# Paced opening loads and whole-piece weight decoding in an attention and two-layer MLP kernel

## The chip, the core and the metric

The kernel runs on one core of a Trainium2 chip. The metric is device time in microseconds (us) of one execution. The core has a matmul engine (TensorE: PE for its matmuls, PEld for its weight loads), VectorE (DVE), ScalarE (ACT), GpSimd (POOL) and SyncE (SP), which issues every DMA of this kernel. Each engine takes its instructions in the order written and stops at the first one whose inputs are not ready.

## The reference

Chunked attention, then two MLPs without biases, in float32:

```python
# attention: batch 4, 8 heads, 768 positions, head_dim 64; chunks of 32 queries
k_full = np.concatenate([mem_k, k_ctx], axis=2)      # 8 memory slots + 16 left + 32 + 8 right
scores = scale * np.matmul(q_c, k_full.transpose(0, 1, 3, 2))
a = np.exp(scores - scores.max(-1, keepdims=True)); a = a / (a.sum(-1, keepdims=True) + 1e-9)
out_c = np.matmul(a, v_full)
x = out.transpose(0, 2, 1, 3).reshape(3072, 512)
# first MLP (w_in 512x2048, w_out 2048x512)
x = np.maximum(x @ w_in, 0.0) ** 2 @ w_out
# second MLP, same sizes, own weights: g(h) = h * tanh(softplus(h))
y = g(x @ w_in2) @ w_out2
```

## The kernel before

**Work.** The 24 tiles of 128 positions are handled as 12 pairs p, four pairs to a superblock `sb` of 1024 tokens (three superblocks). Pairs 0 to 3 are computed in an opening of their own; pairs 4 to 11 are laid beside the first MLP's matmuls. Each MLP layer runs 24 steps, `s` = 0 to 23 for the first and 24 to 47 for the second; a step is one superblock against one eighth `j` of the 2048 hidden columns. Products follow a seven-product (Strassen-like) scheme, so a step has seven products P1 to P7 against w_in (42 matmuls) and, one step later, the products against w_out (48 matmuls, "units", in the first layer).

**One step.** P1 goes to bank a, P6 to b, P5 to c. ACT copies a to `u1`, DVE makes `u2 = b + u1`; then come two units of the step before, P2 (onto a), P7 (onto b), DVE's `u3 = b + u1` (line 835), more units, P4 (onto b), P3 (onto c). P2 has to wait for the copy of a (line 809), P7 for u2 (line 816), P4 for u3 (line 835), and the next step's P6 for DVE's c21 (line 843). Behind every product and unit stands a "point": `rest()` issues there whatever a plan has put at that point of the step (15 points a step).

**Weights.** Weights arrive as 8-byte words and are decoded on the chip: 32 pieces of 128 x 1024 values. Each piece is loaded and decoded in two halves of 512 columns. `rebias` (line 153, ACT) rescales the high words, `decode` (lines 160, 163, 164, DVE) clamps, shifts and adds the low bits. For a w_in piece `sums_w` (lines 175 to 179, DVE) adds the Strassen sums; `round_w` (line 201, ACT) and `split_w` (line 207, DVE) make the two parts that the matmuls use, and for the second layer `round_w2` and `split_w2` (lines 219, 226) write these to DRAM. Three raw buffers hold three halves. The plan string of `plan_w` has one letter for each of these and a bar for each point: `"Aa|D|d|RS|s|rL||||l"`.

**Order.** The scheduler is off (`tc.manual_schedule()`), so the order on each engine is that of the code. In the opening SP issues q, k, v and raw loads one behind the other without waits of the code's own, except where a tile is still in use. PE fills the gaps of the opening with dummy matmuls on `ones` (line 871). Attention beside the first layer puts eight small Exp activations a half (line 403) at two neighbouring points.

Of the kernel before, what the change touches and what calls it, by code (L numbers as in the profile page):

```python
# [26 lines left out]
NB = 512  # L27
# [31 lines left out]
def tile_chunk_attention_moe_moe2(  # L59
# [65 lines left out]
    halves = [(e, h) for e in order_w for h in range(2)]  # L125
    raw_t, val_t, w1_t, w2_t, hi_t = {}, {}, {}, {}, {}
    AHEAD = 3
# [6 lines left out]

    def flush():
        for to, src in waiting:
            nc.sync.dma_start(out=to, in_=src)
        waiting.clear()

    def load_raw(i):  # L140
        if i < len(halves):
            (layer, j, kind), h = halves[i]
            raw_t[i] = pool.tile([128, 512, 2], U32, tag=f"raw{i % AHEAD}", name="raw")
            src = (w1, w2)[layer][j, kind][:, 512 * h:512 * h + 512].bitcast(U32)
            later(raw_t[i], src.rearrange("p (a b) -> p a b", b=2))

    def rebias(e, h, tag):
        i = halves.index((e, h))
        if h == 0:
            flush()  # L150
            val_t[e] = pool.tile([128, 1024 if e[2] and not e[0] else 2048], FP32, tag=tag, name="val")
# [3 lines left out]
    def decode(e, h):  # L155
        i = halves.index((e, h))
        val = val_t[e][:, 512 * h:512 * h + 512]
        vb = val.bitcast(U32)
        low = raw_t.pop(i)[:, :, 0]
# [3 lines left out]
        nc.vector.tensor_scalar(out=vb, in0=vb, scalar1=3, scalar2=None, op0=ALU.logical_shift_left)  # L163
        nc.vector.scalar_tensor_tensor(  # L164
            out=vb, in0=low, scalar=29, in1=vb, op0=ALU.logical_shift_right, op1=ALU.bitwise_or
        )
        load_raw(i + AHEAD)

    def sums_w(e, half):
# [4 lines left out]
        if half == 0:  # L174
            nc.vector.tensor_tensor(out=s1, in0=a21, in1=a22, op=ALU.add)
            nc.vector.tensor_tensor(out=s2, in0=s1, in1=a11, op=ALU.subtract)
        else:
            nc.vector.tensor_tensor(out=s3, in0=a11, in1=a21, op=ALU.subtract)
            nc.vector.tensor_tensor(out=s4, in0=a12, in1=s2, op=ALU.subtract)
# [105 lines left out]
    def spare(sb, i):  # L285

        return f"{('xt', 'raw')[(sb - NSB) % 2]}{i % 3}"

    def load_apart(sb, o):
        xt_t[sb, o] = pool.tile([128, 2 * NB], FP32, tag=spare(sb - 1, 2 * o), name="xa")  # L290
# [793 lines left out]
```

## Time and profile before

| | us |
|---|---|
| median of 3 runs (1087.55 to 1092.18) | 1088.66 |
| the profiled execution's own run | 1090.82 |
| its span in the profile | 1089.0 |

The span is the time from the first to the last instruction in the profiled execution; 1.8 us of its run lie outside it. The opening ends at 56.2 us, where the first product of step 0 starts. In views of the profile, a row of the timeline gives start, duration, engine, source line, operation, what it writes and reads and, in brackets, the engine's idle time ahead of it and what ended that. "issue" there means that no semaphore in the profile ended the wait.

### The profile page before, as it was taken

How to read it: one execution, taken by the hardware profiler on the slowest of the kernel's cores; microseconds unless marked ns; L12 is line 12 of the kernel's file. 1: busy time of each engine (PE TensorE's matmuls, PEld its weight loads, DVE VectorE, ACT ScalarE, POOL GpSimd, SP SyncE). 2: the span in 40 equal slices, each digit the busy share in tenths (PEclk: the TensorE clock that was granted, in tenths of full speed). 3: DMA queues.
4: the chain of work that ended last, by engine and by line, in shares of the span. 5: the costliest groups of instructions: out<-in, count | busy, mean ns of one | idle time of the engine just before them, and what ended most of it. 6: DMA issues, size and time to landing. Idle time of an engine off the chain costs nothing.

```text
span 1089.0 us, 19893 instructions
## 1 busy us (share of the span) xinstructions
PE 1045.6 (96%) x7435; PEld 846.3 (78%) x7443; DVE 847.5 (78%) x1147; ACT 586.5 (54%) x1119; POOL 420.5 (39%) x327
## 2 busy tenths in 40 slices
PE   7878999998999999999999999999999999999998
PEld 4557777776778788788888888888888888888887
DVE  5786979969857676679999767787868878867777
ACT  2567765746675774557565654444364443453332
POOL 1223333332324343222232144545455454644443
PEclk9898998999999999999999999999999999999999
DMA  9556776789999998989999998999998899987452
GB/s 351 222 190 251 270 269 258 273 289 304 350 359 344 326 326 284 300 304 378 352 359 329 312 293 281 312 322 329 387 359 279 295 310 362 376 261 231 152 174 78
DMA packets 192143, 321.38 MB, mean 295 GB/s; under 512 B 13488, under 2 KB 151088, under 8 KB 188208
## 3 DMA queue, kind: packets, MB, share of 16 engines
q1 hardware_dynamic: 192048, 320.11, 84.4%
q8 instruction: 60, 0.98, 0.4%
q14 instruction: 35, 0.29, 0.1%
HBM read 228.04 MB, written 92.01 MB: 294 GB/s over the span
## 4 chain that ended last, share of the span: by engine, by line
PE 59%; DVE 5%; DMA 4%; ACT 2%; SPq 1%; issue 1%; DVEq 0%; ACTq 0%
PE banks L514 28%; PE banks L604 20%; PE banks L569 9%; DMA w_d<-hi 1%; PE banks L647 1%; DMA w_d<-val 1%; DMA xt<-xt_d 1%; DVE y L583 1%; SPq L253 1%; DMA w2s<-w_d 1%; DVE val L164 1%; DVE val L226 1%; DVE val L163 0%; SPq L267 0%; DMA w1s<-w_d 0%
## 5 line engine op out<-in xcount | busy, mean ns | idle before, releaser
L514 PE MATMUL banks<-x,w1s 128*128 128x512 f32 x2016 | 497.5, 393 | 17.4 <-ACT u L809 6.7
L514 PEld LDWEIGHTS banks<-x,w1s 128*128 128x128 f32 x2016 | 378.3, 189 | 103.8 <-DVE u L835 9.5
L528 POOL TENSOR_TENSOR g<-r,g 128x512 fp32r<-128x512 f32 x190 | 263.9, 1396 | 489.6 <-ACT g L527 361.7
L569 PE MATMUL banks<-g,w2s 128*128 128x512 f32 x1152 | 280.1, 393 | 7.0 <-DVE y L583 5.4
L569 PEld LDWEIGHTS banks<-g,w2s 128*128 128x128 f32 x1152 | 215.1, 188 | 57.2 <-DVE y L583 8.3
L592 DVE TENSOR_TENSOR m<-banks,m 128x1024 f32<-128x1024 f32 (+1 forms) x145 | 175.5, 1214 | 51.0 <-PE banks L604 45.8
L604 PE MATMUL banks<-g,w2s 128*128 128x512 f32 x828 | 206.4, 389 | 0.0
L604 PEld LDWEIGHTS banks<-g,w2s 128*128 128x128 f32 x828 | 155.4, 188 | 32.4
L527 ACT CAST g<-r 128x512 fp32r<-128x512 f32 x190 | 115.7, 621 | 27.8 <-DVE r L555 23.3
L583 DVE TENSOR_TENSOR y<-banks,y 128x512 f32<-128x512 f32 x168 | 111.5, 682 | 20.9 <-PE banks L569 20.6
L528 POOL TENSOR_TENSOR g<-more,g 128x512 fp32r<-128x512 f32 x47 | 66.8, 1425 | 63.0 <-ACT g L527 42.2
L533 ACT ACTIVATE r<-r 128x512 f32<-128x512 f32 x72 | 45.4, 630 | 54.7 <-DVE r L843 39.6
L537 ACT ACTIVATE r<-r 128x512 f32<-128x512 f32 x48 | 30.3, 632 | 72.1 <-DVE r L843 37.3
L534 ACT ACTIVATE r<-r 128x512 f32<-128x512 f32 x96 | 60.8, 633 | 3.1
L160 DVE TENSOR_SCALAR val<-val 128x512 f32<-128x512 f32 x64 | 38.6, 603 | 24.8 <-ACT val L153 24.6
L226 DVE TENSOR_TENSOR val<-val,hi 128x1024 f32<-128x1024 f32 (+1 forms) x32 | 35.5, 1109 | 24.0 <-ACT hi L219 23.7
L164 DVE SCALAR_TENSOR_TENSOR val<-raw,val 128x512 uint32<-128x512 uint32 x64 | 50.5, 788 | 2.2
L219 ACT CAST hi<-val 128x1024 fp32r<-128x1024 f32 (+1 forms) x32 | 30.5, 952 | 39.9 <-DVE val L164 18.8
L153 ACT ACTIVATE val<-raw 128x512 f32<-128x512 f32 x64 | 40.4, 672 | 21.1 <-DMA w_d<-val 9.9
L809 ACT COPY u<-banks 128x512 f32<-128x512 f32 x48 | 28.4, 592 | 41.4 <-PE banks L514 41.4
L417 POOL TENSOR_TENSOR p<-p,sum 128x512 f32<-128x512 f32 x22 | 27.6, 1273 | 43.1 <-DVE sum L414 17.6
L835 DVE TENSOR_TENSOR u<-banks,u 128x512 f32<-128x512 f32 x48 | 33.0, 688 | 14.2 <-PE banks L514 11.5
(88 smaller groups left out, 1035.5 us busy)
## 6 DMA issues: line engine op xcount, KB each, us to landing
w1s<-w_d SPq DMA_DIRECT2D x280, 256.0 KB, 6.0
w2s<-w_d SPq DMA_DIRECT2D x229, 256.0 KB, 5.9
raw<-w_dram SPq DMA_DIRECT2D x64, 512.0 KB, 5.8
w_d<-w1s SPq DMA_DIRECT2D x8, 1792.0 KB, 9.2
x<-xs_d SPq DMA_DIRECT2D x14, 1024.0 KB, 11.2
v<-v_dram SPq DMA_DIRECT2D x24, 512.0 KB, 7.6
xt<-xt_d SPq DMA_DIRECT2D x21, 512.0 KB, 8.3
k<-k_dram SPq DMA_DIRECT2D x24, 368.0 KB, 7.2
```

What stands on the lines that cost most here:

```text
L153: nc.scalar.activation(out=val, in_=high.bitcast(FP32), func=ACTF.Prelu, scale=REBIAS, alpha=NEGATIVE)
L164: nc.vector.scalar_tensor_tensor(out=vb, in0=low, scalar=29, in1=vb, op0=ALU.logical_shift_right, op1=ALU.bitwise_or)
L226: nc.vector.tensor_tensor(out=val, in0=val, in1=hi, op=ALU.subtract)
L514: nc.tensor.matmul(out=ps, lhsT=w[:, a, f:f + 128], rhs=x[:, xi, c, kk, :], start=start and i == 0, stop=stop and i == len(order) - 1, ski ...
L527: nc.scalar.copy(out=g[:, 0], in_=r)
L528: nc.gpsimd.tensor_tensor(out=g[:, 1], in0=r, in1=g[:, 0].bitcast(FP32), op=ALU.subtract)
L533: nc.scalar.activation(out=r, in_=h, func=ACTF.Relu)
L534: nc.scalar.activation(out=r, in_=r, func=ACTF.Square)
L569: nc.tensor.matmul(out=ps, lhsT=w[:, a, blk(f), d % 2 * 128:d % 2 * 128 + 128], rhs=g_t[s, (f, t)][:, c, :], start=i == 0, stop=i == len(o ...
L583: nc.vector.tensor_tensor(out=y, in0=ps, in1=y, op=ALU.add)
L592: engine.tensor_tensor(out=to, in0=in0, in1=in1, op=ALU.add)
L604: nc.tensor.matmul(out=bank(first + d), lhsT=w[:, a, 128 * d:128 * d + 128], rhs=g[:, c, :], start=i == 0 and blk not in ONTO, stop=i == 2 ...
```

## The change

Four things change together.

1. In the opening, from the seventh load on, SP first issues a DMA of one element that reads the third load ahead, and so waits until that load has landed; then it issues the load.
2. A weight piece is decoded whole, by instructions of 1024 columns. Its two raw halves lie in one fixed tile `raws` of four halves. The two loads of piece n+2 go out behind the decoding of piece n. `sums_w` needs three instructions for four, and two of its differences change sign (with T3, that they meet).
3. The plans put these instructions at other points: rebias alone at the first, limit two points later, the rest later by a point or two.
4. The Exps of a pair go to four points, four at each; normalisation and the store of a pair move a point or two later. First-layer g tiles use six buffers in a fixed rotation for seven in a ring, which frees room for `raws`.

```diff
-    AHEAD = 3
+    raws = const.tile([128, 4, 1024], FP32, name="raws")
...
-    def rebias(e, h, tag):
...
-        val, high = val_t[e][:, 512 * h:512 * h + 512], raw_t[i][:, :, 1]
-        nc.scalar.activation(out=val, in_=high.bitcast(FP32), func=ACTF.Prelu, scale=REBIAS, alpha=NEGATIVE)
+    def rebias(e, tag):
...
+        val = val_t[e][:, 0:1024].rearrange("p (h f) -> p h f", h=2)
+        high = raw_of(order_w.index(e)).rearrange("p h (f b) -> p h f b", b=2)[:, :, :, 1]
+        nc.scalar.activation(out=val, in_=high, func=ACTF.Prelu, scale=REBIAS, alpha=NEGATIVE)
...
-        load_raw(i + AHEAD)
+        beside_next.append(n + 2)
...
-            nc.vector.tensor_tensor(out=s1, in0=a21, in1=a22, op=ALU.add)
-            nc.vector.tensor_tensor(out=s2, in0=s1, in1=a11, op=ALU.subtract)
+            nc.vector.tensor_tensor(out=s3, in0=a21, in1=a11, op=ALU.subtract)
+            nc.vector.tensor_tensor(
+                out=a[:, 4:6], in0=a[:, 0:7:6], in1=a22.unsqueeze(1).to_broadcast([128, 2, 256]), op=ALU.add
+            )
...
-            3: lambda: (exps(p, 0), load_k(p + 1) if (p + 1) % PSB else None),
-            4: lambda: exps(p, 1),
-            6: lambda: normalize(p),
+            3: lambda: (exps(p, 0, slice(0, 4)), load_k(p + 1) if (p + 1) % PSB else None),
+            4: lambda: exps(p, 0, slice(4, 8)),
+            5: lambda: exps(p, 1, slice(0, 4)),
+            6: lambda: exps(p, 1, slice(4, 8)),
+            7: lambda: normalize(p),
...
+        def paced(*pieces):
+            for issue, piece in pieces:
+                n = len(loads)
+                if n >= 6:
+                    nc.sync.dma_start(out=landed[n:n + 1], in_=loads[n - 3]())
+                issue()
+                loads.append(piece)
...
+        paced(*pieces_q(0), *pieces_k(0), *pieces_q(1), *pieces_k(1))
+        paced(*pieces_v(0), *pieces_raw(0), *pieces_q(2), *pieces_k(2), *pieces_v(1))
+        paced(*pieces_q(3), *pieces_k(3), *pieces_v(2), *pieces_v(3), *pieces_raw(1))
...
-                plan_w(s, 0, (0, s + 1, 0), "Aa|D|d|RS|s|rL||||l", round_w, split_w, "val")
-                plan_w(s, 4, (0, s, 1), "A||a|D|d||R||L", round_w, split_w, "xt2")
+                plan_w(s, 0, (0, s + 1, 0), "A||D|d|RS|s||rL||l", round_w, split_w, "val")
+                plan_w(s, 5, (0, s, 1), "A||D|d||R||L", round_w, split_w, "xt2")
...
-                plan_w(NQ + n, 3, e, "Aa|D|d|RS|s|L|||||r|l", lambda e, i: round_w2(e, i, "xt2"), split_w2, "val")
+                plan_w(NQ + n, 3, e, "A||D|d|RS|s|L||||r|l", lambda e, i: round_w2(e, i, "xt2"), split_w2, "val")
```

Counting q of a pair as one load and k, v and a raw piece as two each, the loads are numbered 0 to 23 in the order of `paced`. On SP, at the seventh load and on, this stood before:

```order
L337 DMA v<-v_dram 128x1024 x2
L137 DMA raw<-w_dram 128x1024 x2
L319 DMA q<-q_dram 128x1024
L324 DMA k<-k_dram 128x736 x2
L337 DMA v<-v_dram 128x1024 x2
```

and this stands there now:

```order
L902 DMA landed<-q 1x1
L353 DMA v<-v_dram 128x1024
L902 DMA landed<-k 1x1
L353 DMA v<-v_dram 128x1024
L902 DMA landed<-k 1x1
L153 DMA raws<-w_dram 128x1024
L902 DMA landed<-v 1x1
L153 DMA raws<-w_dram 128x1024
L902 DMA landed<-v 1x1
L332 DMA q<-q_dram 128x1024
```

Loads keep their order; ahead of each stands a DMA that waits for the third one ahead of it.

On DVE in step 10, from u2 to u3 and the sum behind it before:

```order
L160 TENSOR_SCALAR val<-val 128x512
L163 TENSOR_SCALAR val<-val 128x512
L164 SCALAR_TENSOR_TENSOR val<-raw,val 128x512
L175 TENSOR_TENSOR val<-val 128x256
L176 TENSOR_TENSOR val<-val 128x256
L835 TENSOR_TENSOR u_3718<-banks,u_3551 128x512
L837 TENSOR_TENSOR r<-banks,u_3718 128x512
L178 TENSOR_TENSOR val<-val 128x256
```

(a first half with its own three rows stands ahead of these), and now:

```order
L165 TENSOR_SCALAR val<-val 128x1024
L168 TENSOR_SCALAR val<-val 128x1024
L174 SCALAR_TENSOR_TENSOR val<-raws,val 128x1024
L857 TENSOR_TENSOR u_3598<-banks,u_3451 128x512
L859 TENSOR_TENSOR r<-banks,u_3598 128x512
L185 TENSOR_TENSOR val<-val 128x256
L186 TENSOR_TENSOR val<-val 128x512
```

The u3 addition has moved ahead of the Strassen sums of the weights. In step 0 it moves only ahead of the first split, since the sums there stay in front of it; u2, which stood between the two halves, now stands ahead of the whole decode.

On ACT, from the last g of step 0 to the copy of bank a in step 1, before:

```order
L527 CAST g<-r 128x512
L403 ACTIVATE p,sum<-banks,mneg 128x64 x16
L153 ACTIVATE val<-raw 128x512 x2
L809 COPY u_1154<-banks 128x512
L201 CAST w1s<-val 128x768
```

and now:

```order
L419 ACTIVATE p,sum<-banks,mneg 128x64 x8
L160 ACTIVATE val<-raws 128x1024
L419 ACTIVATE p,sum<-banks,mneg 128x64 x4
L831 COPY u_1147<-banks 128x512
L419 ACTIVATE p,sum<-banks,mneg 128x64 x4
```

The last four Exps have moved behind the copy. In step 4, where the same group of 16 Exps meets the copy, all of them still stand ahead of it (12, the rebias, 4, then the copy).

## Rows read from the trace of the kernel before

**Rows 1.** The page: engines' busy time, share of the span, instructions.

```profile
PE 1045.6 (96%) x7435; PEld 846.3 (78%) x7443; DVE 847.5 (78%) x1147; ACT 586.5 (54%) x1119; POOL 420.5 (39%) x327
```

**Rows 2.** Busy time by stretch: steps 0, 1, 4 and 19.

```profile
core 0: us, PE busy (x) PEld busy (x) DVE busy (x) ACT busy (x) POOL busy (x), PEclk, DMA share, GB/s
56.20:71.76 15.56, 12.27 (x173) 9.06 (x171) 14.07 (x26) 9.22 (x14) 1.91 (x2) 1.00 0.23 76
71.76:104.02 32.26, 26.33 (x227) 20.90 (x226) 23.70 (x35) 25.41 (x67) 9.94 (x8) 0.89 0.71 256
154.10:184.07 29.97, 26.91 (x228) 21.19 (x226) 24.70 (x38) 20.97 (x59) 9.25 (x7) 0.89 0.80 303
513.75:534.15 20.40, 20.40 (x92) 16.89 (x90) 18.89 (x32) 14.12 (x23) 7.70 (x6) 1.00 1.02 378
```

**Rows 3.** Timeline of PE in the opening: scores of pair 2.

```profile
27.20 0.40 PE L367 MATMUL banks<-k,q 64*32 64x64 f32 x23 [2.90 <-issue]
```

**Rows 4.** DMA queues in 24.7 to 26 us: queue, kind, packets, MB, share.

```profile
q8 instruction: 1, 0.02, 4.9%
```

**Rows 5.** Timeline of SP in the opening: q of pair 1, first raw loads.

```profile
4.05 0.43 SPq L319 DMA_DIRECT2D q<-q_dram  x1
...
6.83 1.25 SPq L137 DMA_DIRECT2D raw<-w_dram  x2
```

**Rows 6.** Tile q, the load issued at 4.05.

```profile
DMA to landing us min/median/max: 5.8/5.8/5.8
```

**Rows 7.** Tile raw, the two loads issued from 6.83.

```profile
DMA to landing us min/median/max: 8.8/9.1/9.4
```

**Rows 8.** Tile raw, the twelve loads of 60 to 130 us.

```profile
DMA to landing us min/median/max: 3.8/4.0/6.8
```

**Rows 9.** Busy time by stretch (columns as in rows 2), in the opening.

```profile
10.00:20.00 10.00, 7.33 (x152) 4.28 (x152) 7.84 (x16) 3.81 (x7) 2.04 (x2) 0.83 1.02 403
```

**Rows 10.** Timeline of ACT and of DVE in the opening.

```profile
18.62 1.24 ACT L153 ACTIVATE val<-raw 128x512 f32<-128x512 f32 x2
...
28.42 0.69 DVE L385 TENSOR_REDUCE mx<-banks 128x8 f32<-128x512 f32 x1 [2.58 <-PE banks L367]
```

**Rows 11.** Timeline of DVE and of PE in step 0.

```profile
66.52 0.68 DVE L835 TENSOR_TENSOR u<-banks,u 128x512 f32<-128x512 f32 x1
...
67.26 1.66 PE L514 MATMUL banks<-x,w1s 128*128 128x512 f32 x6 [1.75 <-DVE u L835]
...
74.82 1.45 PE L514 MATMUL banks<-x,w1s 128*128 128x512 f32 x5 [1.54 <-DVE r L843]
```

**Rows 12.** Timeline of ACT and of PE, end of step 0 and step 1.

```profile
78.51 0.31 ACT L403 ACTIVATE p<-banks,mneg 128x64 f32<-128x64 f32 x1
...
84.23 0.68 ACT L809 COPY u<-banks 128x512 f32<-128x512 f32 x1
...
84.97 1.65 PE L514 MATMUL banks<-x,w1s 128*128 128x512 f32 x3 [4.39 <-ACT u L809]
```

**Rows 13.** Timeline of PE in step 4: P7.

```profile
166.07 2.50 PE L514 MATMUL banks<-x,w1s 128*128 128x512 f32 x5 [0.71 <-DVE u L816]
```

**Rows 14.** Waits from 250 to 460 us: us in total, times, longest.

```profile
PE banks L514 <- DVE u L835: 3.5, 5, 1.1
...
PE banks L569 <- DVE y L583: 4.6, 4, 1.5
```

**Rows 15.** Lines 153, 164 and 160, 56 to 460 us: ns min/median/max.

```profile
L153 ACT ACTIVATE val<-raw x44: 647/665/757, 59.3 to 412.6; 128x512 f32<-128x512 f32 x44
L164 DVE SCALAR_TENSOR_TENSOR val<-raw,val x44: 691/693/1777, 61.5 to 418.1; 128x512 uint32<-128x512 uint32 x44
...
L160 DVE TENSOR_SCALAR val<-val x44: 409/426/1297, 60.5 to 416.2; 128x512 f32<-128x512 f32 x44
```

**Rows 16.** Groups by line and form, DVE, 56 to 460 us: busy, mean ns, idle.

```profile
L207 DVE TENSOR_TENSOR w2s<-val,w2s 128x1024 fp32r<-128x1024 f32 x8 | 10.1, 1260 | 0.0
...
L175 DVE TENSOR_TENSOR val<-val 128x256 f32<-128x256 f32 x14 | 7.0, 497 | 0.0
```

More of the change, by code (lines that the diff above doesn't have):

```diff
@@ L124, in tile_chunk_attention_moe_moe2 @@
     order_w += [(1, j, kind) for j in range(NQ) for kind in range(2)]
-    halves = [(e, h) for e in order_w for h in range(2)]
-    raw_t, val_t, w1_t, w2_t, hi_t = {}, {}, {}, {}, {}
-    AHEAD = 3
+    val_t, w1_t, w2_t, hi_t = {}, {}, {}, {}
+    raws = const.tile([128, 4, 1024], FP32, name="raws")
     waiting = []
@@ L133, in later @@
         waiting.append(args)
+    beside_next = []
     def flush():
@@ L138, in flush, with raw_of, load_raw, limit @@
         waiting.clear()
[L140 to L145, printed above, removed]
-    def rebias(e, h, tag):
[L148 to L151, printed above, removed]
-        val, high = val_t[e][:, 512 * h:512 * h + 512], raw_t[i][:, :, 1]
-        nc.scalar.activation(out=val, in_=high.bitcast(FP32), func=ACTF.Prelu, scale=REBIAS, alpha=NEGATIVE)
-    def decode(e, h):
-        i = halves.index((e, h))
-        val = val_t[e][:, 512 * h:512 * h + 512]
+        for n in beside_next:
+            load_raw(n, 0)
+            load_raw(n, 1)
+        beside_next.clear()
+    def raw_of(n):
+        return raws[:, 2 * (n % 2):2 * (n % 2) + 2]
+    def load_raw(n, h):
+        if n < len(order_w):
+            layer, j, kind = order_w[n]
+            src = (w1, w2)[layer][j, kind][:, 512 * h:512 * h + 512]
+            nc.sync.dma_start(out=raw_of(n)[:, h].bitcast(U32), in_=src.bitcast(U32))
+    def rebias(e, tag):
+        flush()
+        val_t[e] = pool.tile([128, 1024 if e[2] and not e[0] else 2048], FP32, tag=tag, name="val")
+        val = val_t[e][:, 0:1024].rearrange("p (h f) -> p h f", h=2)
+        high = raw_of(order_w.index(e)).rearrange("p h (f b) -> p h f b", b=2)[:, :, :, 1]
+        nc.scalar.activation(out=val, in_=high, func=ACTF.Prelu, scale=REBIAS, alpha=NEGATIVE)
+    def limit(e):
+        val = val_t[e][:, 0:1024]
         vb = val.bitcast(U32)
-        low = raw_t.pop(i)[:, :, 0]
         nc.vector.tensor_scalar(
@@ L319, in load_q, with load_k @@
             nc.sync.dma_start(out=q_t[p][half], in_=q[p][half].rearrange("p (t a s) -> p t a s", t=2, a=4))
-    def load_k(p):
-        k_t[p] = pool.tile([128, 2, 4, KCOLS], FP32, tag=f"y{p % 2}" if early(p) else "at0", name="k")
-        for j in range(2):
+    def load_k(p, *halves):
+        if 1 not in halves:
+            k_t[p] = pool.tile([128, 2, 4, KCOLS], FP32, tag=f"y{p % 2}" if early(p) else "at0", name="k")
+        for j in halves or range(2):
             nc.sync.dma_start(out=k_t[p][:, j], in_=k[2 * p + j].rearrange("p (a s) -> p a s", a=4))
@@ L335, in load_v @@
             v_t[p] = [both[:, j] for j in range(2)]
-        for j in range(2):
+        for j in halves or range(2):
             nc.sync.dma_start(
@@ L400, in exps @@
             return
-        m = m_neg.pop((p, h2))
-        for i in range(8):
+        m = m_neg[p, h2]
+        for i in range(8)[part]:
             nc.scalar.activation(
```

87 lines of the change are left out of this document (45 added, 42 removed).

## Prediction

> **What bounds the kernel now.** I read the page first, then the stretches by step, then PE's timeline where steps are too long, and for each idle gap there the engine named in it. PE is busy for 96% of the span and no other engine for more than 78% [rows 1], so time can only come out of places where PE stands or runs slowly. The stretches show where those are. Step 19 takes 20.40 us with PE busy throughout; its 90 matmuls fill it, 0.227 us each [rows 2]. Steps 0, 1 and 4 take 15.56, 32.26 and 29.97 us [rows 2]. Step 0 holds 42 such matmuls and a pair's scores, about 9.5 + 1.5 us, so some 4.5 us are lost in it; in steps 1 and 4 PE is busy for 5.9 and 3.1 us less than the stretch, and the granted clock is 0.89 of full, which costs another 0.11 x 32 = 3.5 and 0.11 x 30 = 3.3 us [rows 2]. Step 19 stands for the steps from 17 on: nothing is left to win there. So the change can act in the opening (56 us) and in steps 0 to 16.
>
> In the opening PE stands for 2.90 us amid the scores of pair 2, and no semaphore ended that wait [rows 3]. One packet of the instruction queue moves in the 1.3 us window that closes 1.2 us before PE resumes [rows 4]. I read this as PE waiting for its next block of instructions. DVE stands for 2.58 us behind it [rows 10]. In the steps PE waits on bank readers: in step 0 for u3 (1.75 us) and c21 (1.54 us), both on DVE [rows 11]; in step 1 for ACT's copy of bank a, 4.39 us [rows 12]; in step 4 for u2 [rows 13]; and between 250 and 460 us five times for u3, 3.5 us in all [rows 14].
>
> **The change, part by part.**
>
> *Pacing.* Before, a raw load in the opening lands 8.8 to 9.4 us after its issue [rows 7], while between 60 and 130 us it lands after 4.0 [rows 8]; the difference is queueing, at 403 GB/s with all DMA engines busy [rows 9]. Now load n is issued when load n-3 has landed, behind one small DMA; an issue takes 0.43 us [rows 5]. A round of three loads then takes about 4.0 + 0.5 = 4.5 us, if the loads are as fast as in rows 8. Load 3 (q of pair 1) lands at 4.05 + 5.8 = 9.9 us [rows 5, 6], and load 9, the second half of the first raw piece, two rounds later: 18.9 us. Before, it lands by about 6.83 + 0.6 + 9.1 = 16.5 us [rows 5, 7]. ACT starts the rescaling at 18.62 [rows 10], so it moves by 0.3 us, and one instruction of 1024 columns gives about that back against 1.24 us for two. Load 12, the last key load of pair 2, lands at 18.9 + 4.5 = 23.4 us, before PE reached the place where it stood until 27.20 [rows 3]. The loads end later, load 23 some 3.7 rounds of 4.5 after load 12, at 40 us, but its piece is decoded beside step 0 at 60 us, 20 us of cover. So the slower loads cost nothing as long as a round stays under about 5.5 us.
>
> What PE's wait of 2.90 us becomes, no row of before tells. Bounds: it stays (0), or it goes with DVE's 2.58 us behind it; the same kind of gain at other blocks makes 4 us a generous end. On the other side a round of 6.8 us, the slowest load of rows 8, puts load 12 at 9.9 + 3 x 7.3 = 31.8 us and costs about 4 us. I take 0: the data's own arrival at 23.4 us is close to where PE already is, and the loads still fill most of the DMA time.
>
> The Trainium skill, page "DMA: Bandwidth & Descriptors", section "Queues, rings and completion order", speaks against a gain here: each DMA engine takes turns between the queues that have work, packet by packet, so a block of instructions should not wait behind the depth of the load queue. By that rule the opening is worth 0 at best; rows 3 and 4 show a late block under full load but not what delayed it.
>
> *Decoding in 1024 columns.* A half takes 0.43 + 0.43 + 0.69 us on DVE [rows 15] by the medians, with line 163 taken like 160, two halves 3.1 us. For the whole piece the row nearest is a 1024-column instruction with two inputs, 1.26 us on average with waits for other engines in it [rows 16]; I take 1.2 for the third instruction and 0.7 for each of the first two (bounds: 0.43, no longer than a half, and 0.86, twice a half). That makes 2.6 us, 0.5 saved a piece. The sums go from four instructions of 256 columns, 0.5 us each [rows 16], to three of 256, 512 and 256; I take 0.2 saved. With 44 halves between 56 and 460 us [rows 15] DVE saves 11 us and a little, but it counts only where PE waits for DVE.
>
> *Order, step 0.* Before, u3 starts at 66.52 [rows 11], behind u2, both halves, the sums and the first split. Now the split (768 columns, 0.95 us by the 1.26 for 1024 of rows 16) stands behind it and the decode is 0.5 shorter, while ACT's single rescaling ends about 0.4 us later than its first half did. I take 0.9 of the 1.75 us. From u3 to c21 the split comes in (0.95), but the decode of the next piece leaves two third instructions, which POOL's work can stretch from 0.69 to 1.78 us [rows 15], for one: 0.5 and one stretch of 1.1 saved, 0.6 in balance. Step 0: 1.5 us (0.5 to 3).
>
> *Order, step 1.* From the first Exp to the copy of bank a ACT takes 84.23 - 78.51 = 5.72 us [rows 12], of which two rescalings are 1.3 and 16 Exps with their sums 4.4, so 0.28 each. Four Exps move behind the copy, 1.1 us, and one rescaling of 1024 columns (bounds 0.67 and 1.33, I take 1.05) saves 0.25. Step 1: 1.3 us of the 4.39 (1 to 3). The remaining idle of 3 us I expect to leave the clock as it is.
>
> *Order, step 4.* All 16 Exps still stand ahead of the copy, but u2 stands ahead of the decode: the 0.71 us go [rows 13]. 0.7 (0 to 5, if DVE's saving in step 3 also shortens the idle ahead of P2).
>
> *Order, steps 8 to 13.* u3 is ahead of the sums and behind a decode that is 0.5 us shorter: 0.5 x 2 + 0.5 = 1.5 us earlier, more than the longest of the five waits, 1.1 [rows 14]. One of the five lies in step 7, where no such piece is decoded ahead of it; I take 2.8 of the 3.5 us (1.5 to 3.5). Of the waits for y, 4.6 us [rows 14], DVE's shorter work takes perhaps 0.7 (0 to 2).
>
> *The rest.* g in six buffers: the two taken at once are free since the step before, the other two after units 0 to 3, which PE has done by then; no wait. Later Exps, normalisation and store have five points of room before the transposes need them. The change of signs costs nothing. Prices of new waits I can't see: 0 to 3 us.
>
> Sum: 0 + 1.5 + 1.3 + 0.7 + 2.8 + 0.7 = 7.0 us less. The profiled execution has a span of 1089.0 us and a run of 1090.82, so it would become 1082.0 and 1083.8; that run is 2.2 us above the median of 1088.66. From the median: 1081.7, rounded to 1081.5.
>
> The Trainium skill has a rule against this part too: "Perfetto Trace Analysis", section "Optimizing Scalar/DVE Operations", says that where VectorE or ScalarE isn't saturated but causes bubbles on other engines, breaking up instructions may let work complete sooner; here they are made longer. By that rule an addition that PE waits for may find 1.2 us of DVE ahead of it for 0.7; it would eat 0.5 us at a wait, and it is the second rival's mechanism below.
>
> **The rivals.** A measurement of this kernel tells about 0.5% from no change, 5.4 us.
>
> 1. *The opening gains* (0.17). With fewer loads queued the blocks of instructions come earlier, and the 2.90 us of PE go with DVE's 2.58 behind them. For it: rows 3 and 4. Against: the loads still arrive at 23.4 us, and then other engines' chains hold. About 3 to 4 us more: 1078.
> 2. *Waits move* (0.28). u3 earlier lets P4 start earlier, but the units behind wait for y, which DVE now adds behind longer instructions; and ACT's cast of the weights, now later, holds the gates. Half of 7 us is left: 1085. For it: the y waits of up to 1.5 us [rows 14]. Against: DVE has 11 us less to do. Here belongs also that the change doesn't do what it says: tiles in use and the queue already space the loads, and order alone decides.
> 3. *The clock stays up* (0.12). If the idle in steps 1 or 4 falls far enough, the 3.5 and 3.3 us at the lower clock go as well [rows 2]: 1074 to 1078. Against: 3 us of idle remain in step 1.
> 4. *Slower* (0.08). A round of the paced loads takes much longer than 4.5 us. Load 12 comes three rounds after 9.9 us, load 17 4.7 rounds after it. At 9 us a round (the landing time of rows 7, at depth) load 12 lands at 37 us for 27.20 now, and the opening ends 10 to 13 us later: 1092 to 1096. It decides from rounds of about 8 us on; against it, the loads of rows 8 land in 4.0 us and only three are in flight.
>
> **How the numbers follow.** My forecast has 0.35 and gives 1081.5 (its own range, 1077 to 1086, from the bounds above). Faster by over 0.5%, below 1083.2: most of the forecast (0.27), rivals 1 and 3 (0.29): 0.56. Within 0.5%: the rest of the forecast, rival 2 and half a chance that rival 4 comes mildly: 0.34. Slower: 0.10. The range leaves one in ten on each side: down to 1071, where rival 1 and 3 meet, up to 1091, where rival 4 begins.
>
> **What would show it.** In the profile after: the opening ends at 56 +- 1.5 us; raw loads land about 4 us after their issue in it; PE's wait of 2.90 us amid the scores of pair 2 is there or not; step 0 takes 14 us, step 1 about 31; waits of PE for u3 between 250 and 460 us fall below 1 us in total; DVE is busy about 15 us less. The prediction is wrong if the opening moves by more than 2 us either way, if steps 1 and 4 run at full clock, or if waits for y or for ACT's casts grow by what u3 gives.

## The result and the profile after

| | before | after |
|---|---|---|
| median of the compared runs, us | 1090.35 (1086.91 to 1092.18, 10 runs) | 1095.94 (1092.04 to 1099.5, 10 runs) |
| the profiled execution's span / run, us | 1089.0 / 1090.82 | 1092.9 / 1094.66 |
| mean granted TensorE clock | 0.989 | 0.986 |

The ratio is 1.0058, with a 95% interval from 1.0041 to 1.0076: the changed kernel is slower by some 6 us, where 7 less were forecast. All tables and runs below give the ratio to the kernel before, measured beside it on the same chip.

Two views of the kernel after answer to [rows 1] and [rows 2]. First the page's engines, then the busy time by stretch: steps 0, 1, 3, 4, 5, 7 and 24.

```profile
PE 1047.7 (96%) x7443; PEld 849.6 (78%) x7443; DVE 828.7 (76%) x1027; ACT 583.0 (53%) x1087; POOL 425.4 (39%) x327
```

```profile
core 0: us, PE busy (x) PEld busy (x) DVE busy (x) ACT busy (x) POOL busy (x), PEclk, DMA share, GB/s
59.27:73.15 13.88, 12.24 (x173) 9.17 (x171) 11.59 (x16) 8.91 (x12) 2.99 (x2) 0.99 0.24 79
73.15:103.23 30.08, 25.96 (x227) 20.56 (x226) 23.45 (x28) 24.46 (x63) 9.81 (x8) 0.94 0.63 223
126.41:155.25 28.84, 27.10 (x357) 22.20 (x356) 20.96 (x30) 15.95 (x25) 11.64 (x9) 0.94 0.67 256
155.25:181.99 26.74, 24.68 (x227) 19.65 (x226) 21.15 (x28) 17.69 (x51) 8.29 (x6) 1.00 0.74 278
181.99:208.74 26.75, 23.78 (x228) 18.85 (x226) 22.00 (x33) 18.64 (x54) 11.84 (x10) 1.00 0.74 272
231.46:259.15 27.69, 23.77 (x91) 18.44 (x90) 16.36 (x20) 12.47 (x18) 5.57 (x4) 0.88 1.01 356
617.03:639.37 22.34, 21.03 (x92) 16.66 (x90) 15.91 (x21) 12.65 (x18) 6.47 (x5) 1.00 0.83 271
```

Steps 0, 1 and 4 are shorter, as forecast and more (13.88, 30.08 and 26.74 us for 15.56, 32.26 and 29.97), and step 4 now runs at full clock. DVE is busy 18.8 us less. Against that, step 0 starts at 59.27 us for 56.20, and steps 3, 5, 7 and 24 have grown: on PE's timeline of before (from the first product of one step to that of the next) they took 27.13, 23.88, 25.50 and 20.40 us. Steps 10 and 15 are longer too, by 1.8 and 1.1 us. So the steps that were expected to gain did, and more than that was lost elsewhere. Three places of loss in the kernel after. The opening, on ACT and on PE:

```profile
19.21 1.13 ACT L160 ACTIVATE val<-raws 128x1024 f32<-128x1024 f32 x1 [1.96 <-DMA raws<-w_dram]
20.24 1.05 ACT L451 COPY pt<-banks 128x512 f32<-128x512 f32 x2
```

```profile
13.04 0.78 PE L383 MATMUL banks<-k,q 64*32 64x64 f32 x56 [1.14 <-issue]
...
20.86 0.30 PE L463 MATMUL banks<-pt,v 64*64 64x32 f32 x4 [3.03 <-ACT pt L451]
...
25.63 0.91 PE L383 MATMUL banks<-k,q 64*32 64x64 f32 x68
```

PE's wait of 2.90 us amid the scores of pair 2 [rows 3] is gone. But ACT's rescaling now waits for the raw load; the copy of `pt`, which PE needs, stands behind it on ACT, and PE waits 3.03 us ahead of the first values. By stretch, the clock falls to 0.83 of full behind that wait, and to 0.66 behind the next one (2.04 us at 32.14, for the copy of pair 1's `pt`; 0.52 us there before):

```profile
20.00:30.00 10.00, 8.96 (x278) 6.51 (x278) 6.96 (x11) 3.83 (x7) 3.49 (x5) 0.83 0.87 281
30.00:40.00 10.00, 7.80 (x264) 6.12 (x264) 4.04 (x8) 4.34 (x7) 5.24 (x6) 0.66 0.85 284
```

Step 5, on ACT, DVE and PE:

```profile
193.72 1.14 ACT L160 ACTIVATE val<-raws 128x1024 f32<-128x1024 f32 x1
...
195.91 0.62 ACT L554 ACTIVATE r<-banks 128x512 f32<-128x512 f32 x1
...
200.27 0.63 ACT L548 CAST g<-r 128x512 fp32r<-128x512 f32 x1
200.80 1.05 ACT L212 CAST w1s<-val 128x1024 fp32r<-128x1024 f32 x1
```

```profile
203.07 0.17 DVE L429 TENSOR_SCALAR sum<-sum 128x16 f32<-128x16 f32 x1 [1.56 <-ACT p L419]
...
203.99 1.80 DVE L218 TENSOR_TENSOR w1s<-val,w1s 128x1024 fp32r<-128x1024 f32 x1
205.71 0.68 DVE L604 TENSOR_TENSOR y<-banks,y 128x512 f32<-128x512 f32 x1
```

```profile
204.13 1.65 PE L590 MATMUL banks<-g,w2s 128*128 128x512 f32 x6 [1.95 <-DVE y L604]
206.44 1.66 PE L590 MATMUL banks<-g,w2s 128*128 128x512 f32 x6 [0.66 <-DVE y L604]
```

The cast of the second part of the weights (L212) has gone behind the next piece's rescaling and the six instructions of two gates (L554 to L548, with Exps between them). On DVE the normalisation (L429) stands at the head until ACT's last Exp is done. The split and the y additions queue behind both, and PE waits for y.

Step 7, on SP and PE:

```profile
229.43 0.38 SPq L489 DMA_DIRECT2D xt_d<-stage  x1
...
241.22 1.20 SPq L278 DMA_DIRECT2D xt<-xt_d  x2
```

```profile
248.85 5.46 PE L535 MATMUL banks<-x,w1s 128*128 128x512 f32 x12 [3.63 <-DVE u L857]
```

The store of pair 7, moved two points later, goes out behind the weights at 229.43 us; the loads of x, which read what it stores, start at 241.22. DVE splits x late, u3 stands behind the split, and PE waits 3.63 us. The twelve matmuls after it take 5.46 us, for 3.01 in the trace of e9 below: the clock has fallen too (0.88 over the step).

### The profile page after: what moved, and what is told of

Its sections match the earlier page's. It is cut to its first block, busy times and chain, and to the rows that moved or that the text cites. A ratio compares the mean times of both kernels' runs of the same rounds, so it can differ in the third digit from the quotient of the medians.

```text
span 1092.9 us, 19741 instructions
## 1 busy us (share of the span) xinstructions
PE 1047.7 (96%) x7443; PEld 849.6 (78%) x7443; DVE 828.7 (76%) x1027; ACT 583.0 (53%) x1087; POOL 425.4 (39%) x327
## 4 chain that ended last, share of the span: by engine, by line
PE 66%; DMA 12%; DVE 10%; ACT 6%; issue 3%; SPq 2%; DVEq 0%; ACTq 0%
PE banks L535 30%; PE banks L625 18%; PE banks L590 14%; DMA w1s<-w_d 2%; PE banks L463 2%; ACT p L419 2%; DVE w1s L218 1%; DMA v<-v_dram 1%; DVE y L604 1%; DVE val L174 1%; DMA w2s<-w_d 1%; DMA xt<-xt_d 1%; DMA xt_d<-stage 1%; DMA x<-xs_d 1%; PE banks L668 1%
## 5 line engine op out<-in xcount | busy, mean ns | idle before, releaser
L590 PEld LDWEIGHTS banks<-g,w2s 128*128 128x128 f32 x1152 | 214.3, 188 | 57.7 <-DVE y L604 8.0
L548 ACT CAST g<-r 128x512 fp32r<-128x512 f32 x190 | 115.9, 622 | 27.7 <-DVE r L576 23.2
L613 DVE TENSOR_TENSOR m<-banks,m 128x1024 f32<-128x1024 f32 (+1 forms) x84 | 101.1, 1209 | 12.8 <-PE banks L625 7.6
L549 POOL TENSOR_TENSOR g<-raws,g 128x512 fp32r<-128x512 f32 x47 | 66.8, 1425 | 63.4 <-ACT g L548 37.2
L554 ACT ACTIVATE r<-r 128x512 f32<-128x512 f32 x72 | 45.5, 632 | 71.0 <-DVE r L865 48.6
L613 DVE TENSOR_TENSOR raws<-banks,raws 128x1024 f32<-128x1024 f32 x40 | 48.9, 1222 | 26.8 <-PE banks L625 26.8
L237 DVE TENSOR_TENSOR val<-val,hi 128x1024 f32<-128x1024 f32 (+1 forms) x32 | 40.3, 1260 | 29.2 <-ACT hi L230 28.6
L838 DVE TENSOR_TENSOR u<-banks,u 128x512 f32<-128x512 f32 x48 | 32.9, 686 | 26.8 <-ACT u L831 21.8
L857 DVE TENSOR_TENSOR u<-banks,u 128x512 f32<-128x512 f32 x48 | 33.1, 689 | 22.5 <-PE banks L535 19.8
L174 DVE SCALAR_TENSOR_TENSOR val<-raws,val 128x1024 uint32<-128x1024 uint32 x32 | 48.6, 1519 | 0.6
L160 ACT ACTIVATE val<-raws 128x1024 f32<-128x1024 f32 x32 | 36.5, 1142 | 22.5 <-DVE y L604 5.5
```

The source lines that it names most:

```text
L160: nc.scalar.activation(out=val, in_=high, func=ACTF.Prelu, scale=REBIAS, alpha=NEGATIVE)
L174: nc.vector.scalar_tensor_tensor(out=vb, in0=low, scalar=29, in1=vb, op0=ALU.logical_shift_right, op1=ALU.bitwise_or)
L237: nc.vector.tensor_tensor(out=val, in0=val, in1=hi, op=ALU.subtract)
L548: nc.scalar.copy(out=g[:, 0], in_=r)
L549: nc.gpsimd.tensor_tensor(out=g[:, 1], in0=r, in1=g[:, 0].bitcast(FP32), op=ALU.subtract)
L554: nc.scalar.activation(out=r, in_=h, func=ACTF.Relu)
```

## The experiments

Medians in us and ratios to before; the median of before was 1088.7 to 1089.5 in these sets. W is the whole-piece decode with its buffers and its moved points, P the pacing, X the Exps at four points with normalisation and store later, "old points" the weights' letters at the points of before.

| run | parts | median | ratio [95% interval] |
|---|---|---|---|
| (after) | W P X | 1095.94 | 1.0058 [1.0041, 1.0076] |
| e1_unpaced | W X | 1095.91 | 1.0053 [1.0034, 1.0071] |
| e2_before_paced | P | 1093.46 | 1.0044 [1.0029, 1.0059] |
| e3_old_exps | W P | 1092.44 | 1.0029 [1.0012, 1.0046] |
| e4_before_new_exps | X | 1090.41 | 1.0010 [0.9993, 1.0027] |
| e5_whole_alone | W | 1090.01 | 1.0002 [0.9990, 1.0014] |
| e6_late_points | W P X, last 9 pieces at old points | 1095.66 | 1.0057 [1.0037, 1.0077] |
| e7_raws_behind | W P X, raws behind k, v, q | 1098.43 | 1.0078 [1.0057, 1.0099] |
| e8_whole_fixed | W, old points, raws behind | 1084.04 | 0.9947 [0.9927, 0.9967] |
| e9_store_back | W P X, store at 22 | 1094.99 | 1.0054 [1.0031, 1.0077] |
| e10_points_alone | W, old points | 1083.42 | 0.9939 [0.9921, 0.9957] |
| e11_fixed_paced | e8 and P | 1086.11 | 0.9965 [0.9951, 0.9978] |
| e12_fixed_pair4 | e8, X for pair 4 alone | 1080.13 | 0.9907 [0.9888, 0.9926] |
| e13_first_points | W P X, w_in pieces of layer 1 at old points | 1088.60 | 0.9996 [0.9977, 1.0016] |
| e14_all_points | W P X, old points | 1087.38 | 0.9981 [0.9965, 0.9997] |
| e15_pair4 | e10, X for pair 4 alone | 1082.42 | 0.9926 [0.9904, 0.9948] |
| e16_paced_raw_first | e11, first raws ahead of v | 1082.68 | 0.9929 [0.9905, 0.9953] |
| e17_cast_back | W P X, second cast at point 5 | 1097.56 | 1.0080 [1.0054, 1.0106] |
| e18_best | e16, X for pair 4 alone | 1081.78 | 0.9940 [0.9917, 0.9963] |

**First set: the parts by themselves** (e1 to e5). e1 takes the pacing out. Of its edit, the lines that act:

```diff
-                if n >= 6:
-                    nc.sync.dma_start(out=landed[n:n + 1], in_=loads[n - 3]())
```

e2 puts `paced` into the kernel before. e3 has the Exps at two points, normalisation at 6 and store at 22 again, e4 puts the new points into the kernel before:

```diff
-            3: lambda: (exps(p, 0, slice(0, 4)), load_k(p + 1) if (p + 1) % PSB else None),
-            4: lambda: exps(p, 0, slice(4, 8)),
-            5: lambda: exps(p, 1, slice(0, 4)),
-            6: lambda: exps(p, 1, slice(4, 8)),
-            7: lambda: normalize(p),
...
-            24: lambda: store_x(p),
+            3: lambda: (exps(p, 0), load_k(p + 1) if (p + 1) % PSB else None),
+            4: lambda: exps(p, 1),
+            6: lambda: normalize(p),
...
+            22: lambda: store_x(p),
```

e5 has the edits of e1 and of e3.

> The changed kernel with its opening loads issued one behind the other, in the same order, without the one-element DMAs that wait for the third load ahead. Theory A, the pacing costs: step 0 started 3.1 us later in the changed kernel than before (59.27 for 56.20) and step 1 still 1.4 us later, and late loads of the next weights follow from it. Then this kernel is 2 to 5 us faster than the changed one, near 1092, and step 0 starts near 56. Theory B, the whole-piece decode and its plan cost (waits for y, for ACT's casts and for u3 in steps 3, 5, 7, 10, 15 and 24): this kernel is within 1.5 us of the changed one, whatever its step 0 does.

> The kernel before, with the pacing of its opening loads alone (halves of weights, plans and Exps as before). Theory A: 2 to 5 us slower than before, near 1093, with step 0 starting 2 to 3 us later. Theory B: within 1.5 us of before.

> The changed kernel with the Exps back at two points, eight at each, and normalisation and store of a pair at their old points. If the Exps at four points are worth what step 1 showed (its length fell from 32.26 to 30.09 us, PE's wait for ACT's copy from 4.39 to 1.49), this is 1 to 3 us slower than the changed kernel. If they push ACT's later work into PE's way (the third theory, C: the waits for ACT's casts, copies and stage of up to 2.6 us in steps 3 to 10 come from the Exps standing later), it is 1 to 4 us faster.

> The kernel before with the Exps at four points, normalisation and store moved as in the change, and nothing else of it. Worth of the Exps: 1 to 3 us faster than before by theories A and B; 1 to 4 us slower by theory C.

> The whole-piece decode with its plan and buffers alone: no pacing, Exps at their old points. Theory B (the decode part costs by itself: 1.9 us in step 24, 1 to 3 us at PE's late block in the last values of the opening): 2 to 4 us slower than before. Rival, the three parts only cost together: within 1 us of before.

No theory holds alone. Pacing costs 0.44% on the kernel before (theory A), but taking it out of the changed kernel gives nothing measurable back (theory B). The moved Exps cost 0.5% on top of W (e5 to e1) and 0.3% on top of W and P (theory C), but nothing sure on the kernel before. W alone is level with before: its gains and its losses cancel. So each part has its own loss to be found, and the parts do not add. The opening of a single trace has to be read with care here: e1 and e5 have the same instructions up to step 0, and it starts at 60.38 us in the trace of e1, at 55.31 in that of e5. In the ten traces that are paced in the changed kernel's order it starts at 57.3 to 62.2 us, in the other seven unpaced ones at 55.3 to 57.7.

**The late pieces and two raw loads** (e6, e7). e6 alters one string, for the last nine pieces; e7 holds the two raw loads that go out at 44 us until k, v and q of pair 4 are issued.

```diff
-                    2 * NQ + 1, 10 * n, e, "A||D|d|RS|s|Lr||l",
+                    2 * NQ + 1, 10 * n, e, "A|D|d|RS|s|Lr||l",
```

```diff
     def flush():
...
+        if hold:
+            return
         for n in beside_next:
...
+        at(0, 0, hold.clear)
```

> The changed kernel with one string altered: the last nine w pieces of the second layer go through limit, decode, sums and casts one point earlier, at the points of before. Theory B: in step 22 the second cast of the last such piece stood behind the two gates of c21 on ACT (0.40 us after step 23's start, for 3.72 us before it), so tile xt2 came free late, and the load, cast and split of x behind it made step 24 22.33 us long. Here the cast stands ahead of the gates again and step 24 takes 20.4 us; the median falls by 1.9 us. Rival: step 24 is late because DVE runs behind in step 22 anyway (its third instruction of 1024 columns takes 2.1 to 2.2 us there), and it stays above 21.5 us.

> The changed kernel with the two raw loads that go out at 44 us moved behind the loads of k, v and q of pair 4. Theory: PE's wait amid the values of pair 3 (1.88 us in the changed kernel, 3.26 without pacing, 0.89 before) is for a block of instructions that moves behind these loads; its packet came at 52.7 to 52.8 us for 51.1 before. With 1 MB less queued ahead of it, the packet comes 1 to 2 us earlier, the wait falls below 1 us, step 0 starts near 57.5 and the median falls by 1 to 2.5 us. Rival: the block comes late for another reason; packet and wait stay as they are.

e6, step 24 by stretch (columns as above):

```profile
617.16:637.57 20.41, 20.41 (x92) 16.89 (x91) 15.04 (x19) 10.40 (x15) 6.26 (x5) 1.00 0.81 257
```

The 22.34 us became 20.41, as the theory had it, though the median shows no 1.9 us (its interval is 2 us to each side). The other traces agree: step 24 takes 22.0 to 22.6 us in all eight that have this string as changed, and 20.4 to 20.5 in the other twelve. In e7 PE's wait amid the values of pair 3, 1.88 us in the changed kernel, is gone, but the median did not fall; it stands above the changed kernel's with overlapping intervals. Taking that wait away gained nothing that shows.

**Both repairs on W alone** (e8, e10). All three strings at the points of before, so that only the merging of the letters is left of the change there (e8 also holds the raw loads back as e7 does):

```diff
-                plan_w(s, 0, (0, s + 1, 0), "A||D|d|RS|s||rL||l", round_w, split_w, "val")
+                plan_w(s, 0, (0, s + 1, 0), "A|D|d|RS|s|rL||||l", round_w, split_w, "val")
...
-                plan_w(NQ + n, 3, e, "A||D|d|RS|s|L||||r|l", lambda e, i: round_w2(e, i, "xt2"), split_w2, "val")
+                plan_w(NQ + n, 3, e, "A|D|d|RS|s|L|||||r|l", lambda e, i: round_w2(e, i, "xt2"), split_w2, "val")
```

> The whole-piece decode alone (no pacing, Exps at old points) with both repairs, and all pieces of the weights of both layers at the points of before. If the points and the place of the raw loads are what the decode part costs: 3 to 5 us faster than the decode part alone, so level with before or up to 2 us faster. If instructions of 1024 columns cost by themselves (PE waits behind longer ones): still 2 us or more slower than before.

> The whole-piece decode without pacing and with old points of the Exps, and the weights' pieces at the points of before; the raw loads at 44 us stay ahead of k, v and q. It tells which of the two repairs made the repaired kernel faster (1084.04 for 1090.01). The points: this one stays near 1084 to 1086. The place of the raw loads: it goes back to 1088 or more.

e8 and e10 are 0.53% and 0.61% faster than before, and with no overlap faster than e5. The place of the raw loads makes no difference; the points do: 1.0002 to 0.9939, 6.6 us by the medians. In all, the whole-piece decode gains as much as the prediction promised, if its pieces stay at their points; where it gains it is another matter, taken up below.

**The points inside the full change** (e13, e14, e17). e13 alters the first of the two strings above and nothing else, e14 all three; e17 moves one letter:

```diff
-                plan_w(s, 0, (0, s + 1, 0), "A||D|d|RS|s||rL||l", round_w, split_w, "val")
+                plan_w(s, 0, (0, s + 1, 0), "A||D|d|RS|sr||L||l", round_w, split_w, "val")
```

> The changed kernel with one string altered: the eight w_in pieces of the first layer at the points of before (limit, decode, sums and first cast a point earlier, second cast two points earlier). In the kernels with all pieces at these points step 5 takes 23.4 us for 25.5 (26.7 in the changed kernel) and step 7 23.4 to 23.9 for 24.9. If the later points of these pieces are the main cost of the change, the median falls by 3 to 5 us, to 1091 to 1093, and PE's waits for y in step 5 go. Rival, the points cost only without the other parts (pacing and the moved Exps hide or replace them): within 1.5 us of the changed kernel, as with the late pieces alone.

> The changed kernel with all three strings at the points of before; pacing, Exps at four points and the moved store stay. If the points' price is the same here as without pacing and Exps (6 us), this is 5 to 7 us faster than the changed kernel, 1089 to 1091, level with before. If the parts mask each other: only 2 to 4 us faster.

> The changed kernel with one letter moved: the second cast of each first-layer w_in piece stands at point 5 instead of 7, so that on ACT it is ahead of the next piece's rescaling and the six instructions of two gates instead of behind them. Everything else of the piece stays a point later than before. Theory D, the cast's place on ACT is the main cause (putting the whole string back gained 6 us): the median falls by 4 to 6 us, to 1089 to 1092, PE's waits of 1.68 us for v in step 3 and of 1.95 us for y in step 5 go or halve. Rival, the later limit, decode and sums cost: within 1.5 us of the changed kernel; the cast would then wait on ACT for the sums of DVE and hold the gates.

One string takes the changed kernel from 1.0058 to 0.9996, 6.7 us (some 3 us to each side); all three to 0.9981. So the points of the seven w_in pieces that are decoded beside the steps are the main cause. e17 refutes theory D, that the cast's place on ACT is enough. Its step 5, on ACT, DVE and PE:

```profile
194.10 1.05 ACT L212 CAST w1s<-val 128x1024 fp32r<-128x1024 f32 x1 [1.36 <-DVE val L190]
```

```profile
203.45 0.18 DVE L429 TENSOR_SCALAR sum<-sum 128x16 f32<-128x16 f32 x1 [3.89 <-ACT p L419]
```

```profile
204.51 1.81 PE L590 MATMUL banks<-g,w2s 128*128 128x512 f32 x6 [2.24 <-DVE y L604]
```

Back in front of the gates, the cast waits 1.36 us for the sums of DVE (L190), all of ACT behind it is late, and DVE stands 3.89 us for the last Exp. In e13 the cast waits as long (1.35 us), but the whole piece is a point earlier: it starts 9.9 us after step 5's first product (187.01 after 177.10), for 11.3 us in e17 (194.10 after 182.81), and PE's waits for y there are 0.85 and 0.65 us for 1.95 and 0.66 in the changed kernel. Both orders with the late decode lose: the cast behind the gates holds the split, the cast ahead of them holds the gates. Over all kept traces with W, step 5 takes 26.7 to 27.8 us with this string as changed and X (six traces), 25.5 with the string alone (two), 24.9 with X alone (two) and 23.3 to 23.4 with neither (seven): in this step the two costs, about 2 and 1.5 us, do add.

In step 3 the same string held a load. The kernel after, on SP and PE, then e13 on SP and PE:

```profile
124.00 0.33 SPq L138 DMA_DIRECT2D w_d<-w1s  x1
124.42 1.27 SPq L353 DMA_DIRECT2D v<-v_dram  x2
```

```profile
135.97 2.40 PE L463 MATMUL banks<-pt,v 64*64 64x32 f32 x128 [1.68 <-DMA v<-v_dram]
```

```profile
121.59 0.33 SPq L138 DMA_DIRECT2D w_d<-w1s  x1
122.01 1.43 SPq L353 DMA_DIRECT2D v<-v_dram  x2
```

```profile
133.18 2.29 PE L463 MATMUL banks<-pt,v 64*64 64x32 f32 x128
```

On SP the load of v stands behind the store of the split weights. With the earlier split it goes out 2.4 us earlier (1.4 of them against the step's start, 126.41 and 125.37), PE's wait for v is gone (the kernel before has one of 1.2 us there), and step 3 takes 25.49 us for 28.85.

**The store and the Exps** (e9, e12, e15). e9 puts the store of a pair back to point 22 and alters nothing else. e12 and e15 take X for pair 4 alone (`if p == PSB`), store at 22.

```diff
-            24: lambda: store_x(p),
+            22: lambda: store_x(p),
```

> The changed kernel with one number altered: the store of a pair stands at its old point, 22 for 24. Theory C in a sharper form, the store's move costs: in step 7 the loads of x for the second superblock can't start before the store of pair 7 has landed; in the changed kernel it is issued behind the next weights at 229.4 us and lands at 241.2, ten microseconds after the step's start, and PE then waits 3.63 us for u3. Here it is issued some 12 us earlier, step 7 takes 25 us for 27.69, step 15 (the same with pair 11) 21.4 for 22.37, and the median falls by 2 to 4 us, to 1092 to 1094. Rival, the Exps' own places cost: steps 7 and 15 stay long, no difference to the changed kernel.

> The repaired whole-piece kernel with the Exps at four points and the normalisation a point later for pair 4 alone, the one whose Exps stood ahead of the copy in step 1; its store stays. Every run with the Exps at four points has step 1 at 30.1 to 30.5 us, the others have 31.0 to 33.1. If that gain stands by itself: 1.5 to 2.5 us faster than the repaired kernel, near 1082. If later steps eat it: level with it.

> The whole-piece kernel with pieces at the points of before and Exps at four points for pair 4 alone, with the raw loads at 44 us in the changed kernel's order. The place of these loads made no difference before (1083.42 and 1084.04): 1079 to 1081.5, level with the kernel that has them behind (1080.13).

e9 on SP:

```profile
220.39 0.33 SPq L489 DMA_DIRECT2D xt_d<-stage  x1
...
233.00 2.81 SPq L278 DMA_DIRECT2D xt<-xt_d  x2
```

The store goes out 9 us earlier, PE's wait of 3.63 us is gone and step 7 takes 23.91 us for 27.69. Step 15 stays at 22.28; that half of the theory is wrong. Other traces bear step 7 out: 25.8 to 27.8 us in the seven with W and the store at 24, 23.4 to 25.0 in the ten with W and the store at 22. In the kernel before the same move costs that step nothing (e4: 25.23 us for 25.50). The median of e9 is 1 us below the changed kernel's, its ratio 0.0004 (0.4 us), each with some 3 us to each side, and the trace kept is of its fastest run: the 3.8 us of the trace do not show in the run times. For pair 4 alone the Exps are worth 0.4% on e8, clear of the noise, but 0.13% on e10 and nothing on e16 (e18 below), both within it: whether they gain by themselves is not settled. Step 1 takes 29.04 us in e12 for 32.34 in e8, PE's wait for the copy of bank a 3.08 for 4.25.

**The pacing** (e11, e16, e18). e11 adds P to e8; e16 alters its order, e18 adds pair 4 to that.

```diff
-        paced(*pieces_v(0), *pieces_raw(0), *pieces_q(2), *pieces_k(2), *pieces_v(1))
+        paced(*pieces_raw(0), *pieces_v(0), *pieces_q(2), *pieces_k(2), *pieces_v(1))
```

> The repaired whole-piece kernel with the pacing of the opening loads put back. Theory A (pacing costs by itself, as in the kernel before, +0.44%): 2.5 to 5 us slower than the repaired one, 1087 to 1089, with the second raw half landing near 19.5 us for 17.4, ACT's rescaling and the copy of pt behind it late, and PE's wait ahead of the first values 2 to 3.5 us. Rival, the repairs absorb it: within 1 us of 1084.

> The repaired paced kernel (1086.11) with the two raw loads of the first piece ahead of the two v loads of pair 0 in the paced order. There the second raw half landed at 20.36 us, ACT's rescaling waited 3.42 us for it, the copy of pt stood behind it, PE waited 4.49 us and then ran 6.8 us at half clock. Theory A, the pacing costs through this one late load: here it lands near 16 us, ACT's wait goes, PE's wait falls below 2 us unless v, now last, takes its place; step 0 starts 1 to 2 us earlier and the median is 1084 or less, level with or better than without pacing. Rival, the lower throughput costs all along the opening: it stays near 1086.

> All that helped together: the whole-piece decode with all pieces at the points of before, the pacing with the first raw loads ahead of v, the Exps at four points for pair 4 alone, the store at its old point. If the gain of pair 4 (3.9 us between the two repaired kernels) adds to the paced kernel with its order mended (1082.68): 1078 to 1081. If both gains are the same time in step 1: 1080 to 1083.

e11, on ACT, on PE, and 20 to 30 us by stretch; then e16, the same:

```profile
20.38 1.12 ACT L163 ACTIVATE val<-raws 128x1024 f32<-128x1024 f32 x1 [3.42 <-DMA raws<-w_dram]
```

```profile
22.03 4.11 PE L466 MATMUL banks<-pt,v 64*64 64x32 f32 x128 [4.49 <-ACT pt L454]
```

```profile
20.00:30.00 10.00, 7.91 (x262) 6.21 (x263) 4.42 (x7) 3.98 (x6) 2.96 (x5) 0.50 0.87 281
```

```profile
17.70 1.13 ACT L163 ACTIVATE val<-raws 128x1024 f32<-128x1024 f32 x1 [1.08 <-DMA raws<-w_dram]
```

```profile
19.84 2.06 PE L466 MATMUL banks<-pt,v 64*64 64x32 f32 x124 [0.18 <-ACT pt L454]
```

```profile
20.00:30.00 10.00, 7.37 (x274) 5.20 (x270) 7.83 (x11) 3.76 (x6) 3.30 (x5) 1.00 0.84 291
```

In e11 ACT waits 3.42 us for the second raw half, PE 4.49 us for the copy behind it, and then all of 20 to 30 us runs at half clock. With the raw loads put ahead of the v loads ACT waits 1.08 us, the stretch runs at full clock, and the kernel goes from 0.9965 to 0.9929 (3 us, with 2 to each side), where the unpaced ones are. So pacing costs through one late load; the lower throughput of the DMAs (281 and 291 GB/s from 20 to 30 us, for 407 in e10, which is unpaced) shows no cost. The trace of e2 has the same chain in the kernel before: ACT waits 1.84 us for the second raw half, PE 3.43 us for the copy behind it. e18 does not add the gain of pair 4 to it, within 2 us. Eight of these kernels beat both the kernel before and the changed one (e8, e10, e11, e12, e14, e15, e16, e18); e12 has the lowest median, 0.93% below before, with an interval that overlaps those of e15 and e16.

## Why the prediction was wrong

**Right.** The cost of an instruction of 1024 columns: limit and shift take 0.685 and 0.695 us and the third 1.226 by the medians between 56 and 460 us, 2.6 us as reckoned. The sums take 0.16 us less a piece, for 0.2, and DVE is busy 18.8 us less for 15. In step 1 PE's wait for the copy of bank a fell from 4.39 to 1.49 us, and the step by 2.2 us for 1.3. In step 4 the wait for u2 is gone. From 250 to 460 us, in the waits of the kernel after, u3 and y both fell [rows 14]:

```profile
PE banks L371 <- ACT stage L475: 2.8, 2, 2.6
PE banks L590 <- DVE y L604: 2.7, 4, 1.2
...
PE banks L535 <- DVE u L857: 1.3, 1, 1.3
```

That makes 2.2 and 1.9 us less, for 2.8 and 0.7. The first line is a new wait, 2.6 us of it in step 10; steps 8 to 13 together are 2.4 us shorter.

**Right in the number, by other ways.** Step 0 is 1.7 us shorter for 1.5, but its wait for u3 fell by 0.2 us alone (1.58 for 1.75), where 0.9 were forecast. What went is a wait that the forecast did not have; before, on PE:

```profile
59.42 6.09 PE L514 MATMUL banks<-x,w1s 128*128 128x512 f32 x24 [1.47 <-ACT x L479]
```

In the trace of e10 it is there as before (1.48 us), and step 0 takes 15.15 us. The wait for c21, counted in step 0, stands in step 1 (74.82 us is past that step's start at 71.76), and it grew from 1.54 to 1.93 us. Of the 3.2 us of step 4, for 0.7, PE's busy time gave 2.2 (26.91 to 24.68 us), with the clock at 1.00 for 0.89: that is rival 3's gain, and the forecast had left it out. And e10, with the merged decode at the old points, came out 6.6 us below before (0.61% of 1089), against a sum of 7.0; that is luck. In its trace steps 3, 4, 5 and 7 give 6.7 us, where the sum had 0.7, while steps 8 to 13 take 1.2 us more, where it had half of its gain, and the waits for u3 from 250 to 460 us are 4.4 us for 3.5. The second layer's string as changed may be what serves u3 there: with it steps 8 to 13 are 1.3 to 3.1 us shorter than before in eight of nine traces, without it, in eight more with W, from 1.2 us shorter to 2.3 longer. It is not shown: no run keeps that string and puts the other two back, and e13 and e14, the nearest pair, are 1.3 and 1.2 us shorter there. Longer instructions cost nothing that shows in e10's total, so the rule that speaks against them (the Trainium skill, "Perfetto Trace Analysis", "Optimizing Scalar/DVE Operations") did not decide the sign here; whether it is at work in the longer u3 waits of e10, no run separates.

**The step that failed: "Prices of new waits I can't see: 0 to 3 us", taken as 0.** The moved letters were priced on DVE alone, between u2, u3 and c21. The first string also moves the second cast from point 5 to 7, on ACT behind a rescaling and two gates. The second split on DVE and the store of w1s on SP keep their points but wait for that cast, and the load of v stands behind the store. The string cost 6.7 us (e13; some 3 to each side), about twice the upper bound; e17 shows that the cast's place alone is not it, the decode and sums a point later belong to it. Rival 2 named ACT's cast, but in the changed kernel the wrong way round, as holding the gates, and let the waits only halve the gain. The time measured lies in the range of rival 4, but not by its mechanism: the rounds of the paced loads were as reckoned, load 12 landed at 23.5 us for 23.4. Of the signs of being wrong, the opening moved by 3.1 us, and step 4, though not step 1, runs at full clock.

**"so it moves by 0.3 us" (pacing, taken as 0).** The landing was right: 18.9 us reckoned, ACT starts at 19.21. Wrong was the 18.62 us it was held against: before, ACT began then because the Exps ahead of it were late, and these because PE had stood in the scores of pair 1:

```profile
14.26 1.02 PE L367 MATMUL banks<-k,q 64*32 64x64 f32 x56 [2.19 <-issue]
```

Pacing shortened that wait to 1.14, ACT was ready at 17.25 (19.21 less its wait of 1.96), and the load was late for it. It cost 0.44% on the kernel before and 0.2 to 0.3% on the repaired one (e11 to e8 and e10, with intervals that overlap). Rival 1 was right in its mechanism: the 2.90 us went. All eight unpaced traces have that wait, of 2.8 to 3.3 us; of the twelve paced ones only e18 has any of it, 0.92 us. "other engines' chains hold" was right too, and one of them had got longer. The Trainium skill ("DMA: Bandwidth & Descriptors", "Queues, rings and completion order") says that a DMA engine takes turns between queues packet by packet; what the prediction drew from it, that pacing has nothing to gain there, did not hold for that wait.

**"Later Exps, normalisation and store have five points of room before the transposes need them."** The transposes are not what reads the store: the x loads of step 7 are, five points behind its new place. That is 3.8 us of step 7 in e9's trace. And the normalisation's first two instructions stand on DVE, where they hold the y additions until the last Exp is done (DVE idles 1.56 us there in step 5; with X that step is some 1.5 us longer).

**Left open.** Why the parts do not add: pacing costs 0.44% alone and 0.05% beside W and X. A late arrival may be absorbed by the next wait, or a wait may bring a stretch at half clock with it; neither was tried apart. Besides, e1's trace opens as late without the pacing as the changed kernel with it (60.38 and 59.27 us), and no run shows whether its other executions do. Nor was the gain from pair 4 settled.

## What to carry to other kernels

When a plan moves a step by a point, follow each of its instructions on each engine's own queue (cast, split, store, and the loads queued behind the store), and ask who reads the result, not who stands next. A start time in a trace is no deadline: ask what held that instruction, since the same change may remove it. When a bundle of edits loses, measure the parts alone and taken out: here a gain of 6.6 us lay under a loss of twice that. And a total that agrees with a forecast does not bear out its terms: hold them against the trace step by step.

## What was not expected of the hardware

The half-clock stretches shown here followed waits of PE and added to them: after a wait of 4.49 us the first 128 value matmuls of e11 took 4.11 us at a granted clock of 0.50, where e16, with a wait half as long, took 2.06 us for 124 of them at 1.00. And kernels scatter by different amounts: the eight runs of e9 lie between 1089.84 and 1100.95 us, the six of e10 between 1081.47 and 1085.59, so that a difference of 2 us in one step of a trace can be lost in the medians.
